# Opening tiles shared between VectorE and GpSimd and put in another order, w and u loaded as rows and transposed

## The chip, the cores and the metric

The kernel runs on one NeuronCore of one Trainium2 chip. A core has five engines that take their instructions in order and wait for each other by semaphores: TensorE (PE), VectorE (DVE), ScalarE (ACT), GpSimd (POOL) and SyncE (SP), and 16 DMA engines. The metric is the device time of one execution in microseconds (us); lower is better. Times of before are three runs and one profiled execution.

## The reference

Three stages follow one another on 3072 tokens of 384 features. The first is a linear attention with a decaying state, for 4 batches, 8 heads, 768 tokens and 48 features a head:

```python
for t in range(S):
    kt, vt, rt = (k[:, :, t], v[:, :, t], r[:, :, t])
    cur = np.einsum('bhd,bhe->bhde', u[None] * kt, vt)
    y[:, :, t] = np.einsum('bhd,bhde->bhe', rt, state + cur)
    state = w[None, :, :, None] * state + np.einsum('bhd,bhe->bhde', kt, vt)
```

w (decay, between 0.85 and 0.95) and u (bonus) have one number per head and feature, 8 x 48. The second stage is `h = x @ w_in; g = h - tanh(h); x = g @ w_out` with 2048 hidden features. The third routes each token to one of 8 experts by cosine similarity and a softmax, and gives `gate * relu(x @ w1[e]) @ w2[e]`.

## The kernel before

The tokens are cut into 24 tiles of 128, a tile object `Att(n)` for each. Attention is done by chunks of 128 tokens: within a chunk by a matrix of scores with a causal mask, between chunks by a state. Powers of w are folded into r and k first. `decay_tables` (L194) makes two tables [112 x 4 x 128] from w: squarings of w (`pw`, L196), a reciprocal, seven doublings (`tab_r`, L206) and a reversed copy on ACT (`tab_k`, L208). 112 partitions hold two heads of 48 features, one from partition 0 and one from 64; four pairs of heads lie beside each other.

The steps of one tile, by method: `products` (L376) multiplies r and k into `rows`; `summed` (L382, L384) sums it with u on PE into `ps_cd` and copies it on ACT to `cd`; `decay_r` (L355) and `decay_k` (L358) apply the tables; `scores` (L423) are 8 matmuls into `pa`, with some fill matmuls on a tile of ones ahead (`fill`, L547, whose results nobody reads); `turned` (L364) transposes k; `diagonal` (L405) makes `am` with cd on its diagonal, 8 instructions on ACT; `causal` (L428) puts the masked scores into `am` on DVE; `values` (L454) multiplies by v; `result_hi` (L459, ACT) and `result_lo` (L462, DVE) write the result in two parts.

Tiles 0 to 2 are made in an opening whose order on every engine is the order in which the code is written (`tc.manual_schedule()`), with 17 warm-up matmuls on PE (L158) ahead. Behind them come three steps (`early`, then `steps`) of the second stage woven with tiles 3 to 5, and then a long body of matmuls for stages two and three. The weights arrive as pairs of numbers in 64 bits, and are converted: bit operations on DVE (L264, L267, L270 to `wraw`), a high part on ACT (L277) and a low part on POOL (L278). One `ffn1` (L557) takes a chunk of such weights, its result `ph` is squared on ACT (`z`, L612, and `q`, L615), joined on DVE (L623, L624) and split (`ghi` L625, `glo` L635). `Logits.turn` transposes the second weights on PE (`pt`, L293) for the routing; `pst` (L475) is the state product of a tile. `IDLE` gives the number of fills ahead of `ffn1` in steps 0 to 5. All DMAs of the opening but u's two are issued by SP: w's two, the columns and rows of tiles 0 to 2 (L333, L334), then embeddings and weights.

Of the kernel before, what the change touches and what calls it, by code (L numbers as in the profile page):

```python
# [29 lines left out]
def rwkv__then__tanh_ffn__then__top1_moe_kernel(  # L30
# [56 lines left out]
    LIST = {0: (), 2: (4, 10), NB - 1: (), NB: (10,)}  # L87
    FA = 6
    START = (0, 1, 2)
    IDLE = (0, 0, 6, 4, 4, 3)  # L90
    CONV = (0, 1, 2, 3, 5, 6, 7, 8, 9, 11, 12, 13, 15, 18)
    nxt = None
    nars = {}
# [51 lines left out]
    nc.vector.memset(pw[:, :, 0:1], 0.5)  # L145
    u_pair = const.tile([PW, HP, 2], F32, name="u_pair")
    nc.vector.memset(u_pair, 0.0)
    for g in range(2):
        nc.sync.dma_start(out=pw[64 * g:64 * g + D, :, 0], in_=w.rearrange("(q g) d -> g d q", g=2)[g])
    for g in range(2):  # L150
        nc.scalar.dma_start(out=u_pair[64 * g:64 * g + D, :, g], in_=u.rearrange("(q g) d -> g d q", g=2)[g])
    ones16 = const.tile([P, P], BF16, name="ones16")
    nc.vector.memset(ones16, 1.0)

    warm = ps.tile([P, 4, P], F32, tag="p", name="warm")

    for _ in range(NWARM):
        nc.tensor.matmul(out=warm, lhsT=ones16, rhs=ones16[:, None, :].to_broadcast([P, 4, P]), start=True, stop=True)  # L158
    ident = const.tile([P, P], F32, name="ident")
    make_identity(nc, ident)  # L160
    ones_f = work.tile([P, P], F32, name="ones_f", tag="z")
    nc.gpsimd.memset(ones_f, 1.0)
    strict = work.tile([P, P], F32, name="strict", tag="q")
# [30 lines left out]
    def decay_tables(between):  # L194
        def square(i):
            nc.vector.tensor_tensor(out=pw[:, :, i + 1:i + 2], in0=pw[:, :, i:i + 1], in1=pw[:, :, i:i + 1],  # L196
                                    op=ALU.mult)

        for i in range(6):
            square(i)  # L200
        nc.vector.reciprocal(out=tab_r[:, :, 0:1], in_=w64)
        for i in range(7):
            n = 1 << i
            if i == 5:
                between()
# [1114 lines left out]
    routing_constants()  # L1320
    for x in st:
        nc.gpsimd.memset(x, 0.0)
    a[1].products(nc.vector)
    a[1].decay_r(nc.vector)
    a[1].decay_k(nc.vector)
# [36 lines left out]
    last = split(*ready[0], i=1)
# [12 lines left out]
    done.add(2)  # L1375
    early.append(ffn1([win(p, 1) for p in range(2)], columns_of(xts[0]), NK, TOK))
# [71 lines left out]
    for i in range(len(steps) + 1):  # L1448
        if i < len(steps):
            j, f = steps[i]  # L1450
            xt = xts[j]
            ph = ffn1([win(p, f) for p in range(2)], columns_of(xt), NK, TOK, IDLE[i] if i < len(IDLE) else 0) \
                if i > 1 else early[2 * i]
            if 0 in accs and spill:
                part = stage(0, [P, TB, DL], F32, "part")
                for t, x in enumerate(accs.pop(0)):
                    nc.scalar.activation(out=part[:, t, :], in_=x, func=AF.Copy)
                spill = False
            parts = squares(ph) if i > 1 else early[2 * i + 1]
# [202 lines left out]
```

## Time and profile before

| | us |
|---|---|
| median of 3 runs | 769.78 (769.21 to 770.74) |
| the profiled execution | 771.22 |
| its span in the trace | 769.6 |
| busy: PE, DVE, ACT, POOL | 756.2, 464.8, 457.1, 300.5 |

The span is the time between the first and the last instruction of the trace, and the profiled execution's own time has 1.6 us around it. PE is busy 98% of the span, warm-up and fill matmuls counted, at a mean granted clock of 0.995 of full speed.

### The profile page before, as it was taken

How to read it: one execution, taken by the hardware profiler on the slowest of the kernel's cores; microseconds unless marked ns; L12 is line 12 of the kernel's file. 1: busy time of each engine (PE TensorE's matmuls, PEld its weight loads, DVE VectorE, ACT ScalarE, POOL GpSimd, SP SyncE). 2: the span in 40 equal slices, each digit the busy share in tenths (PEclk: the TensorE clock that was granted, in tenths of full speed). 3: DMA queues.
4: the chain of work that ended last, by engine and by line, in shares of the span. 5: the costliest groups of instructions: out<-in, count | busy, mean ns of one | idle time of the engine just before them, and what ended most of it. 6: DMA issues, size and time to landing. Idle time of an engine off the chain costs nothing.

```text
span 769.6 us, 15995 instructions
## 1 busy us (share of the span) xinstructions
PE 756.2 (98%) x6143; PEld 718.4 (93%) x6143; DVE 464.8 (60%) x1037; ACT 457.1 (59%) x1064; POOL 300.5 (39%) x362
## 2 busy tenths in 40 slices
PE   9899999999999999999999999999999999999996
PEld 5689899999999999999999999999989999999996
DVE  7967976667656565565555655656684455545430
ACT  5787676655657556656657756768463535544431
POOL 3743680466781671753564341133530202110111
PEclk9899999999999999999999999999999999999999
DMA  8964355243240330232223101052374435454400
GB/s 263 288 206 142 118 170 200 64 165 100 66 148 24 126 122 2 91 94 87 80 69 123 59 32 64 14 171 85 116 229 143 129 115 189 150 173 161 154 31 32
DMA packets 41016, 92.21 MB, mean 120 GB/s; under 512 B 4827, under 2 KB 20597, under 8 KB 39907
## 3 DMA queue, kind: packets, MB, share of 16 engines
q1 hardware_dynamic: 36274, 81.44, 33.0%
q0 software_dynamic: 4240, 9.67, 3.5%
q8 instruction: 50, 0.82, 0.4%
q14 instruction: 36, 0.29, 0.1%
q10 hardware_dynamic: 416, 0.00, 0.0%
HBM read 67.26 MB, written 24.00 MB: 119 GB/s over the span
## 4 chain that ended last, share of the span: by engine, by line
PE 90%; issue 3%; DVE 3%; ACT 2%; DMA 2%; POOL 1%; POOLq 0%; SPq 0%; DVEq 0%; ACTq 0%
PE acc L572 39%; PE ph L557 37%; PE py L454 5%; PE pa L423 3%; DMA eraw<-in_moe_w_dram 2%; PE pt L908 1%; PE warm L158 1%; PE pst L475 1%; POOL out_dram L827 0%; PE pt L293 0%; DVE bits L267 0%; DVE wraw L270 0%; PE pl L303 0%; DVE bits L264 0%; PE accn L1036 0%
## 5 line engine op out<-in xcount | busy, mean ns | idle before, releaser
L557 PE MATMUL ph<-xt,wq 128*128 128x384 f32 (+4 forms) x1712 | 340.1, 341 | 1.9 <-ACT wt L295 1.3
L557 PEld LDWEIGHTS ph<-xt,wq 128*128 128x128 f32 x1712 | 302.7, 188 | 5.9 <-ACT wt L295 1.5
L572 PE MATMUL acc<-wq,ghi 128*128 128x392 f32 (+2 forms) x1120 | 289.1, 343 | 0.9 <-ACT ghi L625 0.9
L572 PEld LDWEIGHTS acc<-wq,ghi 128*128 128x128 f32 (+1 forms) x1120 | 200.3, 187 | 5.9 <-ACT ghi L625 1.2
L572 PE MATMUL acc<-wq,glo 128*128 128x392 f32 (+2 forms) x552 | 182.2, 340 | 0.1
L612 ACT ACTIVATE z<-ph 128x384 f32<-128x384 f32 x128 | 62.8, 490 | 105.0 <-PE ph L557 104.7
L623 DVE TENSOR_TENSOR ph<-ph,z 128x384 f32<-128x384 f32 x128 | 72.0, 563 | 62.6 <-ACT z L612 62.0
L572 PEld LDWEIGHTS acc<-wq,glo 128*128 128x128 f32 (+1 forms) x552 | 102.7, 187 | 0.9 <-DVE glo L635 0.7
L635 DVE TENSOR_TENSOR glo<-ph,ghi 128x384 fp32r<-128x384 f32 x128 | 70.7, 553 | 45.7 <-ACT ghi L625 45.6
L827 POOL DMA_INDIRECT out_dram<-ob,gts x27 | 27.2, 1008 | 176.6 <-ACT ob L917 171.4
L625 ACT ACTIVATE ghi<-ph 128x384 fp32r<-128x384 f32 x128 | 62.6, 490 | 41.0 <-DVE ph L624 37.6
L615 ACT ACTIVATE q<-z,sb_t 128x384 f32<-128x384 f32 x128 | 78.9, 617 | 3.4
L624 DVE SCALAR_TENSOR_TENSOR ph<-q,ph 128x384 f32<-128x384 f32 x128 | 71.7, 560 | 12.5 <-ACT q L615 3.5
L629 ACT ACTIVATE mk<-z,lz_t 128x384 bf16<-128x384 f32 x128 | 77.1, 603 | 0.0
L653 DVE SCALAR_TENSOR_TENSOR glo<-ph,ghi 128x384 fp32r<-128x384 f32 (+2 forms) x56 | 30.7, 549 | 63.8 <-ACT ghi L651 63.8
L651 ACT ACTIVATE ghi<-ph 128x384 fp32r<-128x384 f32 (+4 forms) x56 | 27.5, 491 | 67.6 <-PE ph L557 67.5
L411 POOL TENSOR_TENSOR am<-ident,cd 128x512 f32<-128x512 f32 x36 | 36.8, 1045 | 77.8 <-DVE cd L397 77.1
L886 DVE TENSOR_TENSOR wq<-eraw,wq 128x768 fp32r<-128x768 f32 x60 | 55.1, 955 | 11.5 <-ACT wq L885 11.0
L885 ACT ACTIVATE wq<-eraw 128x768 fp32r<-128x768 f32 x64 | 50.4, 839 | 6.2 <-DMA eraw<-in_moe_w_dram 6.2
L278 POOL TENSOR_TENSOR wq<-wraw,wq 128x768 fp32r<-128x768 f32 (+1 forms) x17 | 30.3, 1782 | 39.6 <-ACT wq L277 38.5
L716 POOL DMA_INDIRECT tab<-tk,irow x24 | 24.4, 1019 | 31.8 <-DVE tk L744 25.1
L491 POOL TENSOR_TENSOR st<-st,pw 112x384 f32<-112x384 f32 x20 | 16.7, 840 | 49.2 <-DVE st L484 43.7
(287 smaller groups left out, 860.0 us busy)
## 6 DMA issues: line engine op xcount, KB each, us to landing
eraw<-in_moe_w_dram SPq DMA_DIRECT2D x32, 768.0 KB, 4.5
rkv<-in_rows_dram SPq DMA_DIRECT2D x18, 640.0 KB, 5.6
tt<-in_cols_dram SPq DMA_DIRECT2D x22, 448.0 KB, 4.4
xd<-xt SPq DMA_DIRECT2D x8, 1152.0 KB, 8.0
wraw<-in_moe_w_in_dram SPq DMA_DIRECT2D x8, 768.0 KB, 8.6
wraw<-in_moe_w_out_dram SPq DMA_DIRECT2D x8, 768.0 KB, 5.2
rkv<-xe SPq DMA_DIRECT2D x22, 192.0 KB, 4.4
xe<-zero SPq DMA_DIRECT2D x2, 1536.0 KB, 15.4
```

What stands on the lines that cost most here:

```text
L454: nc.tensor.matmul(out=self.py[32 * g:32 * g + 32, kk, :], lhsT=lhs, rhs=rhs, start=start, stop=stop)
L557: mark["ph"] = nc.tensor.matmul(out=ph, lhsT=lhs[a][:, kk, :], rhs=rhs(b, kk), start=(kk == 0 and p == 0), stop=(kk == nk - 1 and p == 2)).ins
L572: mm = nc.tensor.matmul(out=acc[t][:lhs.shape[1]], lhsT=lhs, rhs=rhs(b, i), start=(i == span[0] and p == 0), stop=(i == span[1] - 1 and p ...
L612: nc.scalar.activation(out=z, in_=ph, func=AF.Square)
L615: nc.scalar.activation(out=q, in_=z, func=AF.Square, scale=SS, bias=sb_t)
L623: nc.vector.tensor_tensor(out=ph, in0=ph, in1=z, op=ALU.mult)
L624: nc.vector.scalar_tensor_tensor(out=ph, in0=q, scalar=KC, in1=ph, op0=ALU.add, op1=ALU.mult)
L625: mark["ghi"] = nc.scalar.activation(out=ghi, in_=ph, func=AF.Copy).ins
L629: nc.scalar.activation(out=mk, in_=z, func=AF.Relu, bias=lz_t, accum_out=zx[:, step:step + 1])
L635: mark["glo"] = nc.vector.tensor_tensor(out=glo, in0=ph, in1=ghi.bitcast(F32), op=ALU.subtract).ins
L885: nc.scalar.activation(out=hi[c][:, a], in_=t[:, a], func=AF.Copy)
L886: engs[s % len(engs)].tensor_tensor(out=lo[c][:, a], in0=t[:, a], in1=hi[c][:, a].bitcast(F32), op=ALU.subtract)
```

## The change

Five things change. (1) w and u are no longer loaded by element into `pw` and `u_pair`; ACT issues four loads of rows into `wu` [12 x 112], PE transposes them after 6 of the 17 warm-up matmuls, DVE copies w out of PSUM and ACT copies u. SP's first issue is then tile 0's columns. (2) The products of tiles 0 and 1, decay_k of tile 2 and decay_r of tile 3 go from DVE to POOL. (3) The opening is written in another order: decays of tiles 0 and 1 one after the other, sums of tile 2 ahead of values of tile 0, results 0 and 1 behind the third diagonal, the bit operations for the second half of the first weight behind result 2, and the embedding norms later. (4) 13 of the opening's 16 fills go, and the six of step 2. (5) The transposes of the first `Logits` move behind `ffn1` of step 2.

```diff
-    IDLE = (0, 0, 6, 4, 4, 3)
+    IDLE = (0, 0, 0, 4, 4, 3)
...
-    for g in range(2):
-        nc.sync.dma_start(out=pw[64 * g:64 * g + D, :, 0], in_=w.rearrange("(q g) d -> g d q", g=2)[g])
-    for g in range(2):
-        nc.scalar.dma_start(out=u_pair[64 * g:64 * g + D, :, g], in_=u.rearrange("(q g) d -> g d q", g=2)[g])
+    wu = work.tile([3 * HP, PW], F32, name="wu", tag="x2t")
+    nc.vector.memset(wu, 0.0)
+    nc.vector.memset(wu[:HP, D:64], 0.5)
+    for i in range(2):
+        for g in range(2):
+            nc.scalar.dma_start(out=wu[i * (g + 1) * HP:][:HP, 64 * g:64 * g + D],
+                                in_=(w, u)[i].rearrange("(q g) d -> g q d", g=2)[g])
...
+    warming(6)
     ident = const.tile([P, P], F32, name="ident")
     make_identity(nc, ident)
+    ps_wu = ps.tile([PW, 3, HP], F32, tag="p", name="ps_wu")
+    nc.tensor.transpose(ps_wu, wu, ident[:3 * HP, :3 * HP])
+    nc.vector.tensor_copy(out=pw[:, :, 0], in_=ps_wu[:, 0])
+    nc.scalar.activation(out=u_pair, in_=ps_wu[:, 1:].rearrange("p g q -> p q g"), func=AF.Copy)
+    warming(NWARM - 6)
...
-    decay_tables(lambda: a[0].products(nc.vector))
+    routing_constants()
+    decay_tables()
+    for t in a[:2]:
+        t.products(nc.gpsimd)
+    for x in st:
+        nc.gpsimd.memset(x, 0.0)
     a[0].summed()
-    a[0].decay_r(nc.vector)
-    a[0].decay_k(nc.vector)
-    a[0].scores(range(HP), 4)
+    for t in a[:2]:
+        t.decay_r(nc.vector)
+        t.decay_k(nc.vector)
+    a[0].scores(range(HP), 1)
...
     a[0].causal()
-    a[0].values(idle=2)
-    a[0].result_hi()
     a[2].products(nc.vector)
     a[2].decay_r(nc.vector)
-    a[2].decay_k(nc.vector)
+    a[2].decay_k(nc.gpsimd)
     a[2].summed()
-    a[2].scores(range(HP), 2)
+    small_constants()
     a[1].causal()
-    embedding_roots()
-    a[0].result_lo()
+    a[0].values()
     a[2].diagonal(True)
-    a[1].values(idle=3)
+    a[2].scores(range(HP))
+    a[0].result_hi()
+    a[1].values()
     a[1].result_hi()
...
     split(*ready[0], i=0)
+    a[2].values(idle=2)
+    a[1].result_lo()
+    a[2].result_hi()
+    a[2].result_lo()
+    embedding_norms()
     a.append(Att(TB, None))
     a[TB].products(nc.gpsimd)
-    a[2].values(idle=5)
-    a[1].result_lo()
-    a[2].result_hi()
-    for _ in range(2):
-        next(ops)
-    a[2].result_lo()
     for _ in ops:
         pass
...
     a[TB].decay_k(nc.gpsimd)
+    a[TB].decay_r(nc.gpsimd)
...
-    a[TB].decay_r(nc.vector)
...
+            if i == 2:
+                logits[0].turn()
+                done.add(1)
+                load_next()
```

The three places below show the order of instructions on one engine, before and after. Line numbers after the change are 7 to 10 higher for the same line. On DVE at the start of the program, before (`rows` holds the products, `tt` the columns of a tile):

```order
L171 CAST cmask<-strict 128x128
L196 TENSOR_TENSOR pw<-pw 112x4 x6
L201 RECIPROCAL tab_r<-pw 112x4
...
L376 TENSOR_TENSOR rows_162<-tt 112x512
L206 TENSOR_TENSOR tab_r<-tab_r,pw 112x4x32
L206 TENSOR_TENSOR tab_r<-tab_r,pw 112x4x64
L196 TENSOR_TENSOR pw<-pw 112x4
L355 TENSOR_TENSOR tt<-tt,tab_r 112x512
L358 TENSOR_TENSOR tt<-tt,tab_k 112x512
L376 TENSOR_TENSOR rows_162<-tt 112x512
```

and at the same place after:

```order
L167 COPY pw<-ps_wu 112x4
L180 CAST cmask<-strict 128x128
L205 TENSOR_TENSOR pw<-pw 112x4 x6
L210 RECIPROCAL tab_r<-pw 112x4
...
L213 TENSOR_TENSOR tab_r<-tab_r,pw 112x4x32
L213 TENSOR_TENSOR tab_r<-tab_r,pw 112x4x64
L205 TENSOR_TENSOR pw<-pw 112x4
L362 TENSOR_TENSOR tt<-tt,tab_r 112x512
L365 TENSOR_TENSOR tt<-tt,tab_k 112x512
L362 TENSOR_TENSOR tt<-tt,tab_r 112x512
```

The product has left the table chain, and a copy out of PSUM has come ahead of it; the mask cast stands between the copy and the squarings. On POOL in the opening, after (`tk` and `zero` are constants, `st` the states, `first` the columns of tile 2):

```order
L1288 IOTA tk_163 128x48
L383 TENSOR_TENSOR rows_167<-tt 112x512
L1293 MEMSET zero 128x384
L383 TENSOR_TENSOR rows_167<-tt 112x512
L1325 MEMSET st_130 128x384
...
L365 TENSOR_TENSOR first<-first,tab_k 112x512
L285 TENSOR_TENSOR wq_75<-wraw,wq_72 128x384
L383 TENSOR_TENSOR rows_167<-tt 112x512
```

Before, the memsets followed `tk` directly, and the first multiplication on POOL was the low part of the first weight; the two products and decay_k of `first` are new there. On PE at step 2, before:

```order
L364 MATMUL ps_k<-ident,tt 128x112 x4
L293 MATMUL pt<-ident,wraw 128x128 x6
L547 LDWEIGHTS ones_94
L547 MATMUL ph<-ones_94 128x384
L547 LDWEIGHTS ones_94
L547 MATMUL ph<-ones_94 128x384
```

and after:

```order
L371 MATMUL ps_k<-ident,tt 128x112 x4
L564 MATMUL ph<-xt,wq_72 128x384 x2
L564 MATMUL ph<-xt,wq_75 128x384
...
L300 MATMUL pt<-ident,wraw 128x128 x6
L482 MATMUL pst<-first,ktok 48x48 x8
```

The transposes of `wraw` and the fills stood ahead of step 2's `ffn1`; now `ffn1` follows the turn of k directly and the transposes stand behind it.

## Rows read from the trace of the kernel before

**Rows 1.** Windows: stretch, length, busy us (instructions), granted PE clock, DMA share, GB/s.
```profile
core 0: us, PE busy (x) PEld busy (x) DVE busy (x) ACT busy (x) POOL busy (x), PEclk, DMA share, GB/s
0.00:21.30 21.30, 19.44 (x209) 12.42 (x209) 16.60 (x47) 12.23 (x35) 7.41 (x47) 1.00 0.89 264
21.30:37.70 16.40, 13.53 (x100) 11.04 (x101) 16.29 (x35) 12.75 (x35) 12.78 (x10) 0.79 0.99 299
37.70:51.20 13.50, 13.18 (x161) 10.85 (x160) 10.12 (x22) 13.27 (x39) 3.72 (x2) 1.00 0.54 150
...
110.00:769.00 659.00, 652.56 (x5182) 630.33 (x5180) 374.45 (x832) 378.37 (x863) 242.07 (x277) 1.00 0.33 108
```

**Rows 2.** Timeline of the start (start, us, engine, line), and DMA issues to landing.
```profile
1.08 0.89 SPq L149 DMA_DIRECT2D pw<-in_w_dram  x2
1.12 0.89 ACTq L151 DMA_DIRECT2D u_pair<-in_u_dram  x2
1.30 6.64 PE L158 MATMUL warm<-ones 128*128 128x512 bf16 x17 [1.30 <-DVE ones L153]
2.05 0.34 DVE L171 CAST cmask<-strict 128x128 uint8<-128x128 f32 x1 [0.80 <-POOL strict L164]
4.08 1.17 DVE L196 TENSOR_TENSOR pw<-pw 112x4 f32<-112x4 f32 x6 [1.70 <-DMA pw<-in_w_dram]
...
tt<-in_cols_dram SPq DMA_DIRECT2D x2, 448.0 KB, 4.0
...
DMA to landing us min/median/max: 2.4/2.5/2.6
```

**Rows 3.** Timeline: products on DVE and POOL, and tab_k.
```profile
6.48 0.68 DVE L376 TENSOR_TENSOR rows<-tt 112x512 f32<-112x512 f32 x1
7.86 0.63 ACT L208 ACTIVATE tab_k<-tab_r 112x512 f32<-112x512 f32 x1 [4.53 <-DVE tab_r L206]
...
21.85 1.30 POOL L376 TENSOR_TENSOR rows<-tt 112x512 f32<-112x512 f32 x1 [0.47 <-DMA tt<-in_cols_dram]
```

**Rows 4.** decay_r on DVE (ns min/median/max), and decays beside each other on POOL and DVE.
```profile
L355 DVE TENSOR_TENSOR tt<-tt,tab_r x4: 674/692/1402, 7.9 to 31.8; 112x512 f32<-112x512 f32 x4
...
31.33 1.29 POOL L358 TENSOR_TENSOR tt<-tt,tab_k 112x512 f32<-112x512 f32 x1
31.77 1.40 DVE L355 TENSOR_TENSOR tt<-tt,tab_r 112x512 f32<-112x512 f32 x1
```

**Rows 5.** Timeline: one tile's scores, turn, sums and diagonal.
```profile
10.42 0.60 PE L364 MATMUL ps_k<-ident,tt 112*128 112x112 f32 x4
10.86 0.96 PE L382 MATMUL ps_cd<-u_pair,rows 112*128 112x2 f32 x8
11.75 1.16 PE L423 MATMUL pa<-tt 48*128 48x128 f32 x16
...
15.81 0.18 ACT L384 ACTIVATE cd<-ps_cd 128x8 f32<-128x8 f32 x1 [0.41 <-PE ps_cd L382]
16.02 2.45 ACT L405 ACTIVATE am<-ident,cd 128x128 f32<-128x128 f32 x8
```

**Rows 6.** Timeline: embedding norm's power and bit operations in the opening.
```profile
15.75 0.58 POOL L1247 TENSOR_TENSOR en_n<-en_n,half 8x1 f32<-8x1 f32 x1 [8.99 <-DVE en_n L1246]
16.06 0.54 DVE L264 TENSOR_SCALAR bits<-wraw 128x384 int32<-128x384 int32 x1
```

**Rows 7.** Timeline: the waits of ACT and DVE in step 2, and one join.
```profile
37.70 0.90 ACT L277 ACTIVATE wq<-wraw 128x768 fp32r<-128x768 f32 x1 [1.99 <-DVE wraw L270]
...
39.33 0.18 DVE L1260 COPY ent<-ps_en 128x24 f32<-128x24 f32 x1 [1.67 <-PE ps_en L1259]
39.42 0.56 DVE L623 TENSOR_TENSOR ph<-ph,z 128x384 f32<-128x384 f32 x1
```

**Rows 8.** Windows of 2 us with the granted clock, and ffn1 of steps 2 and 3.
```profile
30.00:32.00 2.00, 0.43 (x2) 0.43 (x3) 2.00 (x5) 2.00 (x8) 1.89 (x2) 0.72 1.05 392
32.00:34.00 2.00, 1.14 (x6) 0.73 (x5) 2.00 (x3) 2.00 (x8) 2.00 (x2) 0.50 1.03 394
...
35.73 2.79 PE L557 MATMUL ph<-xt,wq 128*128 128x384 f32 x9
...
44.09 1.89 PE L557 MATMUL ph<-xt,wq 128*128 128x384 f32 x9
```

More of the change, by code (lines that the diff above doesn't have):

```diff
@@ L144, in rwkv__then__tanh_ffn__then__top1_moe_kernel @@
     pw = const.tile([PW, HP, 8], F32, name="pw")
-    nc.vector.memset(pw[:, :, 0:1], 0.5)
     u_pair = const.tile([PW, HP, 2], F32, name="u_pair")
-    nc.vector.memset(u_pair, 0.0)
-    for g in range(2):
-        nc.sync.dma_start(out=pw[64 * g:64 * g + D, :, 0], in_=w.rearrange("(q g) d -> g d q", g=2)[g])
-    for g in range(2):
-        nc.scalar.dma_start(out=u_pair[64 * g:64 * g + D, :, g], in_=u.rearrange("(q g) d -> g d q", g=2)[g])
+    wu = work.tile([3 * HP, PW], F32, name="wu", tag="x2t")
[5 more added lines that the diff above has]
+                                in_=(w, u)[i].rearrange("(q g) d -> g q d", g=2)[g])
     ones16 = const.tile([P, P], BF16, name="ones16")
@@ L155, in rwkv__then__tanh_ffn__then__top1_moe_kernel, with warming @@
     warm = ps.tile([P, 4, P], F32, tag="p", name="warm")
-    for _ in range(NWARM):
-        nc.tensor.matmul(out=warm, lhsT=ones16, rhs=ones16[:, None, :].to_broadcast([P, 4, P]), start=True, stop=True)
+    def warming(n):
+        for _ in range(n):
+            nc.tensor.matmul(out=warm, lhsT=ones16, rhs=ones16[:, None, :].to_broadcast([P, 4, P]), start=True, stop=True)
+    warming(6)
     ident = const.tile([P, P], F32, name="ident")
     make_identity(nc, ident)
+    ps_wu = ps.tile([PW, 3, HP], F32, tag="p", name="ps_wu")
[3 more added lines that the diff above has]
+    warming(NWARM - 6)
     ones_f = work.tile([P, P], F32, name="ones_f", tag="z")
@@ L192, in small_constants, with decay_tables @@
         nc.vector.memset(ent, 0.0)
-    def decay_tables(between):
+    def decay_tables():
         def square(i):
@@ L203, in decay_tables @@
             n = 1 << i
-            if i == 5:
-                between()
             nc.vector.tensor_tensor(out=tab_r[:, :, n:2 * n], in0=tab_r[:, :, 0:n],
@@ L1312, in rwkv__then__tanh_ffn__then__top1_moe_kernel @@
     a = [Att(n, xts[0]) for n in range(TB)]
-    decay_tables(lambda: a[0].products(nc.vector))
+    routing_constants()
[4 more added lines that the diff above has]
+        nc.gpsimd.memset(x, 0.0)
     a[0].summed()
-    a[0].decay_r(nc.vector)
-    a[0].decay_k(nc.vector)
-    a[0].scores(range(HP), 4)
+    for t in a[:2]:
+        t.decay_r(nc.vector)
+        t.decay_k(nc.vector)
+    a[0].scores(range(HP), 1)
     a[0].turned()
     a[0].diagonal(True)
[L1320 to L1325, printed above, removed]
     a[1].summed()
@@ L1329, in rwkv__then__tanh_ffn__then__top1_moe_kernel @@
     a[1].diagonal(True)
-    small_constants()
-    embedding_norms()
     a[0].causal()
-    a[0].values(idle=2)
-    a[0].result_hi()
     a[2].products(nc.vector)
     a[2].decay_r(nc.vector)
-    a[2].decay_k(nc.vector)
+    a[2].decay_k(nc.gpsimd)
     a[2].summed()
-    a[2].scores(range(HP), 2)
+    small_constants()
     a[1].causal()
-    embedding_roots()
-    a[0].result_lo()
+    a[0].values()
     a[2].diagonal(True)
-    a[1].values(idle=3)
+    a[2].scores(range(HP))
+    a[0].result_hi()
+    a[1].values()
     a[1].result_hi()
@@ L1349, in rwkv__then__tanh_ffn__then__top1_moe_kernel @@
     a[2].causal()
+    a[0].result_lo()
     next(ops)
     split(*ready[0], i=0)
+    a[2].values(idle=2)
[3 more added lines that the diff above has]
+    embedding_norms()
     a.append(Att(TB, None))
     a[TB].products(nc.gpsimd)
-    a[2].values(idle=5)
-    a[1].result_lo()
-    a[2].result_hi()
-    for _ in range(2):
-        next(ops)
-    a[2].result_lo()
     for _ in ops:
         pass
+    embedding_roots()
     last = split(*ready[0], i=1)
@@ L1490, in rwkv__then__tanh_ffn__then__top1_moe_kernel @@
             logits.append(Logits(c, ready[2 * c + 1][0]))
-            logits[c].turn()
-            done.add(2 * c + 1)
+            if c:
+                logits[c].turn()
+                done.add(2 * c + 1)
         if m < NF:
```

## The prediction

> **What bounds the kernel now.** I read the table of windows first, with borders at the end of the hand-ordered opening (21.3 us), at the second weight conversion of step 2 on ACT (37.7 us) and at the point from which PE is hardly ever idle (51.2 us) [rows 1]. From 110 us to the end PE is busy 652.56 of 659 us at the full granted clock. The change touches nothing there, so whatever it moves before about 51 us comes through to the end whole, as an earlier or later start of a PE-bound body. Before that the limits differ by stage. To 21.3 us PE works 19.44 us, but a part of that is warm-up and fill matmuls. From 21.3 to 37.7 us DVE is busy 16.29 of 16.40 us: DVE sets the pace, and a microsecond that DVE starts later or gets more of is a microsecond. From 37.7 to 51.2 us ACT is busy 13.27 of 13.50 us and PE 13.18.
>
> Then I read the timeline of the opening, to see what each engine waits for. DVE starts the six squarings of the decay at 4.08 us, once the last load of w has landed; the tables are its only work, apart from tile 0's products [rows 2, 3]. ACT sits idle 4.53 us until tab_k at 7.86 us. From then on ACT makes three diagonals of 2.45 us each with short waits between them for PE's small sums (0.41 us before the third), and the third ends at 16.02 + 2.45 = 18.47 us [rows 3, 5]. Causal mask, values, result and the first ffn1 follow from that.
>
> **The loads and the tables.** Before, two loads on SP and two on ACT run side by side. After, ACT issues four. Two issues take 0.89 us there and begin at 1.12 us, so the fourth begins at about 1.12 + 3 × 0.445 = 2.45 us, and with 2.5 us to landing (2.4 to 2.6 for u) it lands at 4.95 us [rows 2]. The new loads have rows of 48 floats in place of single elements; a landing 0.7 us sooner is my optimistic end, since no row shows such a small load landing under 2 us. The transpose costs about 0.15 (a quarter of the four in ps_k, 0.60), the copy 0.18 (as the ent copy), and the mask cast, which DVE now does between copy and squares, 0.34 [rows 2, 5, 7]. Squares start at about 5.65 with a hand-over, say 5.7, in place of 4.08. The table chain ran from 4.08 to 7.86 with one product of 0.68 in it, that is 0.60 by start to start, so 3.16 us without it. Undisturbed it ends at 5.7 + 3.16 = 8.9: 1.0 us later than before, the saved product included.
>
> **The products on POOL.** A product takes 1.30 us on POOL against 0.68 on DVE [rows 3]. SP's first issue is now tile 0's columns: 1.08 + 4.0 = 5.1 us landed, and POOL makes product 0 from 5.1 to 6.4 us [rows 2]. Product 1 follows behind a memset, in any case before the tables end. So both lie beside DVE's table work. What that costs is the disputed price. The trace has one clear place: decay_r of 112x512 takes 0.69 us (median of four), but 1.40 us where it began 0.44 us into a POOL multiplication of the same shape [rows 4]. It lost 0.71 us of the 0.85 that POOL still had to run, nearly the whole of it. The bounds are therefore zero (the small 112x4 operations slip in between) and a full block: 0.7 us for product 0 (5.7 to 6.4) and 1.3 for product 1, together 2.0. I take the full price, because the one place where two such streams meet shows it. Tables then end at 8.9 + 2.0 = 10.9, 3.0 us later than tab_k began before.
>
> The Trainium skill, page "SBUF — State Buffer", section "Who interferes with whom", speaks against this part of the change: a DVE instruction with two SBUF inputs and a GpSimd instruction that reads SBUF exclude each other, the second to issue blocks fully, and issue order rather than shape decides who blocks. By that rule small operations are no way out, and the sum would be the one with 2.0; the trace agrees for the large shape (1.40 against 0.69), and no run here shows it yet for 112x4.
>
> **From the tables to the third diagonal.** Decays r and k of tile 0 are 2 × 0.69 behind the tables (tab_k's 0.63 beside the first): scores 0 at 12.3. PE then needs scores 1.16, ps_k 0.60 and ps_cd 0.96 before ACT can start cd of tile 1: 12.3 + 2.72 = 15.0; its diagonal, with cd, takes 2.45 + 0.18: 17.7. In the new order the sums of tile 2 stand on PE directly behind tile 1's scores and turn (15.0 + 2.72 = 17.7), not behind values 0, so the third diagonal ends at 17.7 + 2.65 = 20.35 instead of 18.47: **+1.9 us** [rows 5]. The removed fills cost or give nothing here: PE waits for tables in their place. The product of tile 2 and its decay_r fit on DVE while ACT works; decay_k of tile 2 on POOL takes 1.3 us while PE does tiles 0 and 1, and is covered so long as it is done by about 16 us.
>
> **DVE behind the opening.** Before, the bit operations on the second half of the first weight (L264, L267) sat in DVE's wait for result 2. Now they stand behind it: 2 × 0.54 = 1.1 us. The embedding norms also come later: DVE's part, 0.1, and a power of 0.58 on POOL that DVE then waits for, of which I count 0.5. Against it, decay_r of tile 3 leaves DVE (0.67, about 0.6 by start to start) [rows 4, 6]. Net **+1.1 us**, in the stretch in which DVE has no idle time to swallow it.
>
> **Step 2.** Six fills go, and the six weight transposes move behind ffn1. PE had sat there waiting for DVE's wraw, the granted clock fell to 0.72 and 0.50 of full speed, and ffn1 took 2.79 us instead of 1.89 [rows 8]; ACT waited 1.99 us for wraw and DVE 1.67 for what came after [rows 7]. After, ffn1 no longer waits for the transposes, so its z and what follows can fill ACT's wait. At most 1.99 us come back. At the low end DVE now has to fit two operations of 0.56 (L623, L624 of step 2) ahead of that same wraw, which leaves 1.99 − 1.1 = 0.9. I take **−1.2 us**, nearer to the low end, since DVE is the engine that this stretch waits for [rows 1].
>
> Sum: 1.9 + 1.1 − 1.2 = +1.8 us. The profiled execution took 771.22 us (span 769.6), so 773.0; it stood 1.44 above the median of 769.78, so the median should be **771.6 us**. From there the PE-bound body keeps the shift.
>
> **The rivals.** Faster or slower by 0.2% is 1.54 us, about what a measurement of this kernel can tell from no change: below 768.24 or above 771.32.
>
> A, the forecast: POOL's products stretch the tables. 771.6, own range 770.6 to 772.6. Chance 0.40.
>
> B: the block does not bite, because small operations slip past or the products start outside the tables. Tables end at 8.9, decays at 10.3; but PE's eleven warm matmuls behind the transpose, at 6.64 / 17 = 0.39 each, end at 5.1 + 4.3 = 9.4, then ps_cd 0.96 and one fill, so scores 0 at 10.6. Twice 2.72 gives sums of tile 2 at 16.05, third diagonal at 18.75: +0.3. With +1.1 and −1.2 the sum is +0.2: 770.0. For it: the table operations last only 0.16 to 0.4 us, and the trace shows the block on longer ones. Chance 0.25.
>
> C, the other side: ACT's diagonals set the opening and nothing else does. If the row loads land by about 4.2 us and nothing blocks, squares start by 4.9, warm-up ends at 4.2 + 0.15 + 4.3 = 8.65, cd 0 starts at 9.6 at the latest, and three diagonals back to back take 3 × 2.63 = 7.9: they end at 17.5, or 17.1 if PE hands over sooner, because the 0.4 us waits of ACT for the sums are gone with the sums of tile 2 moved forward. That is −1.0 to −1.4 against 18.47. ACT then also takes its whole 1.99 in step 2: −1.1 + 1.1 − 2.0 = −2.0, so 767.8. It decides from the point at which the tables end before about 8.2 us. Against it: four issues in a row on one queue. Chance 0.20.
>
> D: the clock. PE idles from 1.30 + 6 × 0.39 = 3.6 to 5.0 us for the transpose and from about 10.4 to 12.3 for the late scores, with fewer fills. In the trace, where PE had 0.43 us of work in 2 us, the clock fell, and one ffn1 cost 0.9 us more [rows 8]. Once or twice that on top of A: 772.5 to 773.4, middle 773.0. Chance 0.15.
>
> **Range and chances.** A lies around the upper bound, more above it (0.26) than within (0.14). B: 0.18 same, 0.04 faster, 0.03 slower. C: 0.15 faster, 0.05 same. D: slower. So faster 0.19, same 0.37, slower 0.44. The range runs from just under C's value to D's upper end, 767.6 to 773.4; it leaves out half of C's spread and the far tail of D, some 0.17.
>
> **What would show it.** In the changed trace: squares starting near 5.7 (if under 4.9, C lives); table operations on DVE with an idle or stretched time of 0.7 and 1.3 us exactly beside POOL's two products (if each keeps its 0.16 to 0.4 us, B); third diagonal ending near 20.4; the first ffn1 near 23.2 instead of 21.35; granted clock 1.00 through the opening (else D); no window at half clock around 32 to 37 us, and z of step 3 some 1.8 us later than before. I am wrong if the block is a matter of large shapes only, if the loads by rows land much faster, or if the bit operations find another gap on DVE.

## The result and the profile after

The changed kernel took 778.32 us (median of 6 runs, 776.42 to 781.10), the kernel before 769.50 on the same chip (6 runs): ratio 1.0111, 95% interval 1.0085 to 1.0136. It is slower by 8.8 us, where 1.8 was forecast. The profiled execution took 781.10 us (span 779.4) and is the slowest of the six, so its trace shows more loss than the median run has. Runs of this kernel spread over 4.7 us and the mean granted clock of a run goes from 0.982 to 0.993, the lowest of them in the slowest run.

The windows of the profile after, cut at scores 0 (14.9 us), the first ffn1 (31.2, the place of the first border of [rows 1]) and z of step 3 (57.3):

```profile
core 0: us, PE busy (x) PEld busy (x) DVE busy (x) ACT busy (x) POOL busy (x), PEclk, DMA share, GB/s
8.50:14.90 6.40, 4.20 (x18) 2.11 (x16) 5.91 (x19) 1.32 (x5) 1.74 (x5) 0.77 1.03 357
14.90:31.20 16.30, 15.71 (x170) 13.65 (x170) 9.07 (x21) 8.97 (x30) 2.11 (x2) 0.58 0.82 235
31.20:57.30 26.10, 21.89 (x179) 18.69 (x183) 22.18 (x49) 21.04 (x58) 19.22 (x14) 0.87 0.48 147
57.30:110.00 52.70, 51.04 (x501) 47.08 (x501) 43.83 (x95) 37.89 (x94) 25.45 (x20) 1.00 0.47 146
```

Scores 0 start at 14.9 us, and the first ffn1 comes 16.3 us behind them, at a mean granted clock of 0.58. In the windows of before the same two points lie 12.0 us apart, at full clock:

```profile
9.30:21.30 12.00, 11.44 (x181) 8.84 (x180) 11.20 (x25) 9.88 (x32) 1.53 (x2) 1.00 1.03 322
21.30:46.00 24.70, 21.81 (x185) 17.77 (x189) 21.88 (x47) 20.88 (x56) 14.63 (x11) 0.86 0.81 240
```

So by the first ffn1 the loss is 31.2 − 21.3 = 9.9 us, of which 5.6 lie ahead of scores 0 and 4.3 behind them. Another 1.4 comes in steps 2 and 3 (26.1 against 24.7). From z of step 3 on the shift stays: 46.04 to 57.30, and 53.66 to 64.90 for the next one. The end is only 9.8 us later, since PE's wait behind late expert weights near 521 us of before (0.9 us) is not there after; the other 0.5 us lie in the same 20 us and were not followed further. That wait comes and goes with runs of either kernel: in the twenty profiles PE waits 0 to 1.2 us there, and from z of step 3 to the end it takes between 721.75 (e5) and 724.50 us (e9), 723.56 in before. So z of step 3 shows what the opening costs more cleanly than the end of one execution does.

The start of the program, as timeline of after (start, us, engine, line), answers to [rows 2, 3]; the last line is a piece of the chain of work (start, us, what).

```profile
1.19 0.85 ACTq L151 DMA_DIRECT2D wu<-in_w_dram  x2
2.06 0.66 ACTq L151 DMA_DIRECT2D wu<-in_u_dram  x2
7.37 0.19 PE L166 MATMUL ps_wu<-ident,wu 12*112 12x12 f32 x1 [3.14 <-DMA wu<-in_u_dram]
7.55 1.26 POOL L383 TENSOR_TENSOR rows<-tt 112x512 f32<-112x512 f32 x1 [0.96 <-DMA tt<-in_cols_dram]
7.68 2.65 DVE L180 CAST cmask<-strict 128x128 uint8<-128x128 f32 x1
8.75 1.49 POOL L1325 MEMSET st<- 128x384 f32 x4
13.48 0.63 ACT L215 ACTIVATE tab_k<-tab_r 112x512 f32<-112x512 f32 x1 [5.51 <-DVE tab_r L213]
14.89 2.08 PE L430 MATMUL pa<-tt 48*128 48x128 f32 x16 [2.20 <-DVE tt L365]
...
2.40 4.83 DMA wu<-in_u_dram
```

Three things are to be seen. The fourth load was issued at 2.40 us, as forecast (2.45), but took 4.83 us to land, not 2.5; tile 0's 448 KB, issued at 0.92, and three more loads that SP had issued by then were ahead of it. The cast took 2.65 us, not 0.34: POOL's product 1 and the four memsets of `st` lie beside it, and it ends when the last memset does. And PE waited 2.20 us for the scores' operand, after which the same 16 matmuls took 2.08 us instead of 1.16.

The clock in windows around that wait:

```profile
12.00:14.00 2.00, 0.70 (x6) 0.45 (x5) 1.83 (x7) 0.52 (x1) 0.00 (x0) 1.00 1.06 386
14.00:16.00 2.00, 1.10 (x10) 1.11 (x12) 2.00 (x4) 1.90 (x8) 0.00 (x0) 0.72 0.90 351
16.00:28.00 12.00, 12.00 (x106) 10.77 (x108) 5.36 (x15) 5.67 (x21) 1.72 (x1) 0.50 0.76 221
```

PE was idle for 2.2 us, then the granted clock fell from 2.4 to 1.2 GHz, and stayed there for at least 12 us in which PE was busy without a gap. In those 12 us everything of the opening stands behind PE. (The 0.77 ahead of scores 0 in the first table is an earlier fall, to 0.51 from 8 to 10 us, behind PE's 3.14 us wait for the transpose. It met the warm-up; PE was through with its sums and its fill at 12.70 us, before the scores' operand was there.)

### The profile page after: what moved, and what is told of

It reads as the page before. It is cut to its first block, busy times and chain, and to the rows that moved or that the text cites. A ratio compares the mean times of both kernels' runs of the same rounds, so it can differ in the third digit from the quotient of the medians.

```text
span 779.4 us, 15967 instructions
## 1 busy us (share of the span) xinstructions
PE 760.0 (98%) x6125; PEld 724.1 (93%) x6125; DVE 464.9 (60%) x1034; ACT 456.7 (59%) x1065; POOL 306.5 (39%) x366
## 4 chain that ended last, share of the span: by engine, by line
PE 90%; issue 3%; DVE 3%; DMA 1%; ACT 1%; POOL 1%; ACTq 0%; POOLq 0%; DVEq 0%
PE acc L579 39%; PE ph L564 38%; PE py L461 5%; PE pa L430 4%; PE pt L915 1%; PE pst L482 1%; PE pt L300 1%; DMA wu<-in_u_dram 1%; DMA eraw<-in_moe_w_dram 1%; PE pl L310 1%; PE ps_cd L389 1%; POOL out_dram L834 0%; DVE bits L274 0%; DVE wraw L277 0%; PE ps_k L371 0%
## 5 line engine op out<-in xcount | busy, mean ns | idle before, releaser
L435 DVE COPY_PREDICATED am<-cmask,pa 128x512 f32<-128x512 uint8 x48 | 33.0, 733 | 6.5 <-PE pa L430 4.8
## 6 DMA issues: line engine op xcount, KB each, us to landing
xd<-xt SPq DMA_DIRECT2D x8, 1152.0 KB, 11.9
```

## Experiments

All ratios are to the kernel before on the same chip, from 4 to 12 runs a kernel. The table gives the ratio with its interval, and from each profile the starts of the first ffn1 and of z of step 3 (before 21.35 and 46.04, after 31.21 and 57.30). It lies near the ratio of the mean times, so a long run moves it: e12 has 1.0073, but 1.0054 by its medians, with one run of seven at 781.08 us; e7 has 1.0045, and 1.0066 by its medians.

| run | ratio | first ffn1 | z of step 3 |
|---|---|---|---|
| e1_w_first | 1.0080 (1.0067 to 1.0093) | 26.52 | 52.54 |
| e2_cast_early | 1.0075 (1.0052 to 1.0098) | 25.32 | 51.32 |
| e3_products_dve | 1.0095 (1.0080 to 1.0110) | 25.28 | 51.31 |
| e4_step2_as_before | 1.0115 (1.0100 to 1.0129) | 31.13 | 56.25 |
| e5_before_step2 | 0.9997 (0.9985 to 1.0009) | 21.23 | 46.95 |
| e6_elements | 1.0049 (1.0032 to 1.0066) | 25.53 | 51.47 |
| e7_three | 1.0045 (1.0024 to 1.0065) | 24.93 | 51.37 |
| e8_three_fills | 1.0050 (1.0032 to 1.0067) | 30.08 | 54.53 |
| e9_fills | 1.0086 (1.0067 to 1.0105) | 27.16 | 51.70 |
| e10_before_less_fill | 1.0003 (0.9985 to 1.0021) | 25.81 | 50.06 |
| e11_before_products | 1.0025 (1.0005 to 1.0044) | 21.77 | 46.09 |
| e12_before_rows | 1.0073 (1.0047 to 1.0099) | 25.84 | 50.87 |
| e13_more_warm | 1.0039 (1.0025 to 1.0054) | 22.30 | 47.73 |
| e14_order | 1.0005 (0.9996 to 1.0013) | 21.74 | 47.10 |
| e15_before_hold | 1.0007 (0.9998 to 1.0016) | 21.43 | 45.87 |
| e16_late_and_lock | 1.0084 (1.0070 to 1.0097) | 26.96 | 52.43 |
| e17_rows_on_sp | 1.0078 (1.0058 to 1.0097) | 27.66 | 53.73 |
| e18_step2_held | 0.9984 (0.9970 to 0.9997) | 21.37 | 43.95 |

**The late loads.** Four runs change part (1) alone, e1 and e17 only the issue of its loads, e6 and e12 the transpose and the warm-up in two parts too; three are on the changed kernel and one on the kernel before.

```diff
# e1_w_first: SP issues w's rows ahead of tile 0's columns
-            nc.scalar.dma_start(out=wu[i * (g + 1) * HP:][:HP, 64 * g:64 * g + D],
+            (nc.sync, nc.scalar)[i].dma_start(out=wu[i * (g + 1) * HP:][:HP, 64 * g:64 * g + D],
# e17_rows_on_sp: SP issues all four
+            nc.sync.dma_start(out=wu[i * (g + 1) * HP:][:HP, 64 * g:64 * g + D],
# e6_elements: loads by element into pw and u_pair as before, no transpose, 17 warm-up matmuls in a row
# e12_before_rows: the kernel before with the new loads, transpose and warm-up in two parts
```

> The changed kernel with w's two row loads issued by SP ahead of tile 0's columns and u's two by ACT; nothing else differs. Late load (the small loads wait 4.83 us behind SP's big ones): the last row lands near 4.1 us instead of 7.23, squares start near 5, tables end between 8.2 and 9.7 instead of 13.5, the first ffn1 starts near 22 to 24 instead of 31.2, time 769 to 772. Lock (POOL's products hold DVE off wherever the tables lie): tables shift by the same 3 us only, the stretched 2.5 us moves to another table operation, time 774 to 776. Clock alone (too few fills): half clock stays from the first scores on, time above 775.

> The changed kernel with all four row loads issued by SP, one after the other, ahead of tile 0's columns; nothing else differs. If the big loads ahead make the small ones late: the last row lands near 4.8 us (issue near 2.3, 2.5 to landing) in place of 7.23, squares start near 5.4, ratio 1.004 to 1.009 as in the run with w first. If four issues in a row on one queue make them late: landing near 7 and ratio 1.010 or more.

> The changed kernel with part (1) undone: w by element on SP ahead of tile 0's columns, u by element on ACT, no transpose, 17 warm-up matmuls in a row; POOL's products, order, fills and step 2 stay changed. Late load as the main cause: squares at 4.1 us, tables end near 8.7 (one block of 1.3 by product 0), and the ratio falls from 1.011 to 1.000 to 1.004. Lock and missing fills as main causes: tables near 9.5, PE idle ahead of scores 0, half clock behind it, ratio 1.006 to 1.009.

> The kernel before with part (1) alone: w and u by rows from ACT, the transpose, tile 0's columns leading SP; products stay on DVE, fills and order as before. Late load alone: the last row lands near 7.2, squares start near 7.9 with the cast at its 0.15 to 0.34 us, scores 0 start near 13.2, and since PE has its eleven late warm-up matmuls and the fills in between the clock stays: ratio 1.004 to 1.006. If the row load is late only with POOL's products beside it: landing near 5, ratio 1.000 to 1.002.

In e17 the four issues stand in a row on one queue, the last at about 2.3 us as in the changed kernel, but ahead of the columns. Its timeline:

```profile
1.18 0.73 SPq L151 DMA_DIRECT2D wu<-in_w_dram  x2
1.96 0.63 SPq L151 DMA_DIRECT2D wu<-in_u_dram  x2
2.63 0.32 SPq L340 DMA_DIRECT2D tt<-in_cols_dram  x1
...
4.16 0.23 PE L166 MATMUL ps_wu<-ident,wu 12*112 12x12 f32 x1
```

The transpose starts at 4.16 us, right behind the six warm-up matmuls and without a wait for a load. So the last of them, issued at about 1.96 + 0.63 / 2 = 2.28, had landed at most 1.9 us later, and it was not the four issues but the big loads ahead. Nor was it ACT's queue: in e1 ACT issues u's rows, the second at about 1.6 us, tile 0's columns follow on SP at 1.96, and the transpose does not wait either (4.15 us). e12 shows the same from the other side, in a kernel in which POOL reads nothing there: issued at 2.40 us, landed 5.54 us later, as the chain has it.

```profile
2.40 5.54 DMA wu<-in_u_dram
...
8.38 0.22 DVE L180 CAST cmask<-strict 128x128 uint8<-128x128 f32 x1
8.52 1.17 DVE L205 TENSOR_TENSOR pw<-pw 112x4 f32<-112x4 f32 x6
```

With late loads alone, transpose and warm-up in two parts included, z of step 3 is 4.8 us later, and the ratio 1.0073. The queueing was shown by the order of issue; how the engines share packets among queues was not measured. e1 (777.18 us, where 769 to 772 was expected) and e6 (1.0049, where 1.000 to 1.004 was) did not come down to what the late-load theory alone expected; e17 lies within its range, and e12 above it with an interval that reaches into it. In e1, e6 and e17 PE still waited ahead of scores 0 (2.81, 2.19 and 2.30 us), and the clock fell in the opening.

**DVE and POOL.** Three runs take the overlap away or bring it alone.

```diff
# e2_cast_early: the cast of cmask stands ahead of the copy of w
+    nc.vector.tensor_copy(out=cmask, in_=strict)
     nc.vector.tensor_copy(out=pw[:, :, 0], in_=ps_wu[:, 0])
# e3_products_dve
-    for t in a[:2]:
-        t.products(nc.gpsimd)
...
+    a[0].products(nc.vector)
...
+    a[1].products(nc.vector)
# e11_before_products: the kernel before with
+    for t in a[:2]:
+        t.products(nc.gpsimd)
```

> The changed kernel with DVE's mask cast ahead of the copy of w out of PSUM, so that it runs near 2 us; nothing else differs. Lock: the cast takes 0.34 us again, the first square now waits for product 1 (to 8.8 us) and the memsets do not stretch it, tables end near 12.0 instead of 13.5, time 776 to 777. If memsets on POOL hold DVE off as well, the first square is stretched as the cast was, tables end at 13.3 and the time stays at 778. Late load alone: 778.

> The changed kernel with products 0 and 1 on DVE, each ahead of its tile's decays, and POOL's memsets directly behind the constants; nothing else differs. Lock: cast and squares are no longer stretched (0.34 and 1.17 us), tables end near 11.2, and with the product on DVE the scores start near 13.4 instead of 14.9: time 776 to 777. Late load alone: scores 0.7 later than in the changed kernel, time 778 to 779.

> The kernel before with products 0 and 1 on POOL ahead of its memsets, the fills kept; loads, order and step 2 as before. Lock: product 0 lies at 6.0 to 7.3 beside the last table operations and holds one of them to its end, product 1 at 8.9 to 10.2 does the same to a decay, and scores 0 start at 9.8 to 10.2 instead of 9.3; with PE's fills as cover the ratio is 0.999 to 1.002. No lock: scores 0 start at 8.7, ratio 0.998 to 1.000.

In e1 the tables are early and still beside the products. Two single operations of its timeline, each with the product that lies beside it:

```profile
5.62 1.26 POOL L383 TENSOR_TENSOR rows<-tt 112x512 f32<-112x512 f32 x1 [0.29 <-DMA tt<-in_cols_dram]
5.68 1.22 DVE L205 TENSOR_TENSOR pw<-pw 112x4 f32<-112x4 f32 x1
...
8.09 1.26 POOL L383 TENSOR_TENSOR rows<-tt 112x512 f32<-112x512 f32 x1 [1.21 <-DMA tt<-in_cols_dram]
8.25 1.25 DVE L213 TENSOR_TENSOR tab_r<-tab_r,pw 112x128 f32<-112x128 f32 x1
```

A square of 112x4 that takes 0.17 us alone took 1.22, until the product was over; a doubling of 112x128 that takes 0.29 took 1.25. Together that is 2.0 us, the full price that I had taken: small operations are held like large ones. In e2 the cast ran at 2.05 us in 0.33, and the squares met product 1 and then the memsets:

```profile
7.49 1.26 POOL L383 TENSOR_TENSOR rows<-tt 112x512 f32<-112x512 f32 x1 [0.75 <-DMA tt<-in_cols_dram]
7.84 1.94 DVE L205 TENSOR_TENSOR pw<-pw 112x4 f32<-112x4 f32 x6
8.69 1.49 POOL L1325 MEMSET st<- 128x384 f32 x4
9.81 0.18 DVE L210 RECIPROCAL tab_r<-pw 112x4 f32<-112x4 f32 x1
```

Six squares take 1.17 us in e12 and 1.94 here: 0.8 us longer, which is what was left of the product (8.75 − 7.84 = 0.91, less what one square does in it). The memsets, from 8.69 to 10.18, cost them nothing. So the cast, with one input, is held by product and memset, and a square, with two inputs, by the product alone. In e9 and e16, with the same order on both engines, the cast did not wait for the last memset: it ended at 9.66 and 9.31 us, and there the four memsets took 1.57 us instead of 1.49, until 10.37 and 10.03. The Trainium skill, page "SBUF — State Buffer", section "Who interferes with whom", has both halves: an operation with two SBUF inputs is in the way of a GpSimd instruction that reads SBUF, not of one that only writes, and a DVE instruction in a two-port mode, which a copy or a cast can enter, of any. The trace agrees with it on both counts (1.94 against 1.17, 2.65 against 0.22); that the cast runs in such a mode is not in the trace. e3, without products on POOL, has the cast at 0.22 us and scores 0 at 13.16 instead of 14.89; e2 has them at 13.33. In the times neither run is clear of the changed kernel: the intervals of 1.0075 and 1.0095 overlap with its 1.0085 to 1.0136. z of step 3 comes 6 us sooner in both profiles, but most of that is the clock: from scores 0 to the first ffn1 they take 12.0 and 12.1 us against 16.3. It is down for about 3 us there and for 13 in the profile after, and it falls near 18 us, with PE busy since scores 0, so not every fall stands right behind a wait.

e11 brings the products alone to the kernel before: scores 0 start at 9.71 instead of 9.33 and z of step 3 is where it was, with a ratio of 1.0025 that its interval hardly sets apart from 1. With the tables early, the price does not reach z.

**The clock.** Five runs change what PE does while it waits.

```diff
# e9_fills: the changed kernel with fills 12, 2, 2, 3, 5 (e10: the kernel before with 1, 0, 0, 0, 2)
-    a[0].scores(range(HP), 1)
+    a[0].scores(range(HP), 12)
# e7_three: e1, e2 and e3 together; e8_three_fills: and fills 4, 2, 2, 3, 5
# e13_more_warm: e8 with step 2 as before, and
-    warming(NWARM - 6)
+    warming(20)
```

> The changed kernel with the opening's fills put back (2, 2, 3, 5) and 12 fills ahead of scores 0, enough to cover PE's wait for the late tables; loads, products and order stay as changed. Clock: tables still end near 13.5 and scores 0 start near 14.9, but no half clock follows, so from scores 0 to the first ffn1 it takes 12 to 12.7 us as before instead of 16.3, first ffn1 near 27.3, ratio 1.005 to 1.008. If the clock does not matter there (ACT or DVE set the pace): first ffn1 stays past 30, ratio 1.010 to 1.012.

> The kernel before with the opening's fills cut as in the change (1, 0, 0, 0, 2); nothing else differs. If the fills alone hold the clock: half clock appears between 12 and 20 us, first ffn1 at 23 or later instead of 21.35, ratio 1.002 to 1.006. If the clock falls only with the late tables: clock stays at 1.00, PE gets up to 2 us ahead and waits, first ffn1 at 20.5 to 21.4, ratio 0.998 to 1.000.

> The changed kernel with three edits at once: w's row loads on SP ahead, the mask cast ahead of the copy, products 0 and 1 on DVE. Late load and lock together: squares at 4.6 with 1.17 us, tables end near 7.9, scores 0 near 9.9, first ffn1 near 21.5 to 22.5, ratio 1.000 to 1.003. If missing fills alone suffice for the fall of the clock: scores start early, but half clock appears between 12 and 22 us, first ffn1 after 24, ratio above 1.005.

> The changed kernel with w's row loads on SP ahead, the mask cast early, products 0 and 1 on DVE, and the opening's fills as before (4, 2, 2, 3, 5); left of the change are row loads with the transpose, the order, and step 2. If late load, lock and clock are the whole loss of the opening: squares near 4.6, scores 0 near 10.0, no half clock to 25 us, first ffn1 near 21.5 to 22.3, z of step 3 near 47 to 48, ratio 1.000 to 1.003. If the new order itself costs something: first ffn1 past 23, ratio 1.004 to 1.006.

> The kernel of e8_three_fills (w's loads ahead, cast early, products on DVE, fills as before) with 20 instead of 11 warm-up matmuls behind the transpose and step 2 as before; left of the change are row loads with the transpose and the order. If the clock explains the rest: PE has no gap of over 1 us ahead of scores 0, full clock to 25 us, first ffn1 near 21.5 to 22.5, ratio 0.999 to 1.002. If the order costs something by itself: first ffn1 past 23 at full clock, ratio 1.003 or more.

Windows of e9, from the warm-up to scores 0, from there to the first ffn1, and on to z of step 3:

```profile
8.90:15.20 6.30, 6.30 (x29) 3.32 (x27) 5.82 (x20) 2.28 (x8) 1.47 (x4) 1.00 1.05 373
15.20:27.10 11.90, 11.35 (x181) 8.77 (x180) 8.37 (x19) 7.93 (x26) 2.43 (x2) 1.00 0.82 221
27.10:51.70 24.60, 20.72 (x179) 17.79 (x183) 22.27 (x49) 21.14 (x58) 17.00 (x14) 0.93 0.60 181
```

Scores 0 are as late as ever, but PE was busy through the wait, the clock is at 1.00 from there on, and the stretch to ffn1 took 11.9 us instead of 16.3. That settles 4.3 us of the profile on the clock. The 1.00 of the first row is not to be trusted for the warm-up, which does not run faster there than in the changed kernel at 0.51 (the first line is e9, the second after):

```profile
8.00:10.00 2.00, 2.00 (x6) 0.75 (x5) 1.91 (x4) 0.07 (x1) 2.00 (x5) 1.00 1.05 297
8.00:10.00 2.00, 2.00 (x7) 0.69 (x6) 2.00 (x2) 0.00 (x0) 2.00 (x5) 0.51 0.96 263
```

From scores 0 on the matmuls bear it out: the sixteen take 1.16 us, as before.

In the times e9's 1.0086 against 1.0111 lies within the intervals. The clean pair is e4 and e16, which differ in fills alone: 1.0115 (1.0100 to 1.0129) and 1.0084 (1.0070 to 1.0097), 0.3% or 2.4 us apart, z of step 3 at 56.25 and 52.43, and a mean granted clock of 0.983 to 0.988 in e4's four runs, of 0.992 to 0.995 in e16's five. The same stretch of the opening in e4 and in e16, where PE gets through 36 and 79 instructions:

```profile
20.00:24.00 4.00, 4.00 (x36) 3.70 (x38) 2.47 (x4) 1.63 (x6) 0.15 (x1) 0.50 0.95 264
20.00:24.00 4.00, 4.00 (x79) 2.77 (x81) 2.75 (x5) 2.89 (x11) 0.05 (x1) 1.00 0.93 267
```

The clock does not fall in every execution. Of e10's twelve (768.6 to 774.2 us) two, at 774.2 and 774.0, have a mean granted clock of 0.984 and 0.985, the other ten 0.990 to 0.995. Three of those ten took 772.3 to 774.1 all the same, as four of 25 runs of before did on that chip (772.3 to 773.3), so the clock is not the whole of the spread. e10's profile is the slowest run and has half clock from 12 to 24 us:

```profile
8.00:10.00 2.00, 1.19 (x17) 0.94 (x18) 1.97 (x4) 1.90 (x7) 0.00 (x0) 1.00 1.09 258
10.00:12.00 2.00, 2.00 (x22) 1.88 (x18) 2.00 (x9) 1.16 (x4) 0.00 (x0) 0.82 1.00 236
12.00:14.00 2.00, 2.00 (x17) 1.91 (x17) 1.97 (x4) 1.72 (x7) 0.00 (x0) 0.50 1.06 390
```

There PE had waited 0.60 us for the product and 0.81 ahead of scores 0, with one fill in place of four. So with these fills cut the clock fell in some executions and not in others, and the ratio of 1.0003 shows no cost in the mean. e7, too without them, has four runs with a mean granted clock of 0.991 to 0.993, three of them at 769.9 to 770.3 us, and seven with 0.984 to 0.987, at 773.4 to 776.4. With fills (e8) six of seven are at 0.992 to 0.995, and take 771.7 to 775.1; in e8's profile, its slowest run, PE waited 1.85 us for product 0 behind its shorter warm-up and the clock fell for the whole opening. With nine more warm-up matmuls (e13) it stayed at 1.00 to 30 us, and the first ffn1 came at 22.30. Its ratio of 1.0039 is above what its z of step 3 (+1.7 us, 0.2%) says; where the rest lies I have not settled.

**Step 2, and the order.** Five runs.

```diff
# e4_step2_as_before: the changed kernel without the hunks for IDLE and logits[0].turn()
# e5_before_step2: the kernel before with both; e18_step2_held: with the second, IDLE[2] = 6, and in turn()
+                fill(pt, 0 if self.c else 4)
# e15_before_hold: the kernel before with fills of 9 and 5 there, IDLE[2] = 2
# e14_order: the changed kernel with loads, products, fills and step 2 as before
# e16_late_and_lock: the changed kernel with e9's fills and step 2 as before
```

> The changed kernel with step 2 as before (six fills, transposes ahead of ffn1); nothing else differs. As forecast in the prediction, step 2 gives 0.9 to 2.0 us back, so without its change the time rises to 779 to 780.5. Rival: the moved transposes make PE wait for the results of the diagonal instead, so that the clock falls there (0.50 from 50 to 55 us), and without the change the time falls by 1 to 2 us, to 776.5 to 777.5.

> The kernel before with step 2's change alone (no fills there, transposes behind ffn1). My prediction's term: 0.9 to 2.0 us faster, ratio 0.9975 to 0.999. Rival, from the runs so far (first ffn1 to z of step 3 took 26.0 us with the change of step 2 and 25.1 without it): 1 us slower at z of step 3, ratio 1.000 to 1.002.

> The kernel before with step 2's transposes behind its ffn1, the six fills ahead of ffn1 kept, and four more ahead of each half of the transposes. If the change of step 2 is worth something with the clock held: no window under 0.9 between 30 and 46 us, z of step 3 at 45.3 to 45.6 instead of 46.04, ratio 0.9985 to 0.9997. If the clock falls all the same, or ACT and DVE set the pace: z of step 3 at 46 to 47, ratio 0.9997 to 1.002.

> The kernel before with fills ahead of step 2's transposes (9 and 5) and 2 instead of 6 ahead of its ffn1, so that PE is busy from 29.7 to 35 us. If the fall of the clock there costs time: ffn1 of step 2 takes 1.9 us instead of 2.8, z of step 3 comes 0.5 to 1.0 us sooner, ratio 0.9985 to 0.9995. If ACT and DVE set the pace there: z of step 3 at 46.0, ratio 0.9995 to 1.0005.

> The changed kernel with loads, products of tiles 0 and 1, fills and step 2 as before; what is left is the new order, decay_k of tile 2 and decay_r of tile 3 on POOL. My prediction's term for DVE behind the opening is +1.1 us and the third diagonal no later than before: ratio 1.001 to 1.002. The rival by which sums of tile 2 ahead of values 0 free ACT: third diagonal ends up to 1.4 us sooner, ratio 0.998 to 1.000.

> The changed kernel with 12 fills ahead of scores 0, the other fills as before, and step 2 as before; loads, products and order stay changed. If the parts add up: z of step 3 some 4.5 us later than before (5.5 with the fills alone, 1.0 less for step 2), ratio 1.005 to 1.007. If step 2's change matters only when the clock falls in the opening: 5.5 us, ratio 1.007 to 1.009.

In the profiles of the changed kernel and of e5, step 2's part makes z of step 3 later, by 57.30 − 56.25 = 1.05 and 46.95 − 46.04 = 0.91 us. The times show neither: 1.0111 with it and 1.0115 without (e4), and 0.9997 for e5. ffn1 of step 2 itself comes sooner, as meant, but PE then waits for DVE, 1.63 and 0.65 us for `causal`, and the clock falls at the scores and transposes ahead of ffn1 of step 3. From the windows of after:

```profile
50.00:52.00 2.00, 2.00 (x16) 1.48 (x17) 2.00 (x6) 1.99 (x8) 1.86 (x1) 0.50 0.80 316
52.00:54.00 2.00, 2.00 (x19) 1.52 (x11) 2.00 (x4) 1.77 (x6) 0.00 (x0) 0.50 0.02 8
54.00:56.00 2.00, 2.00 (x8) 1.50 (x7) 0.11 (x1) 1.32 (x4) 1.52 (x1) 0.54 0.29 36
```

PE is full there and DVE at the end nearly idle. e18 keeps six fills ahead of that ffn1 and puts four ahead of each half of the transposes. Its window of the same work, from the first ffn1 to z of step 3, and z itself:

```profile
21.30:43.90 22.60, 20.41 (x197) 17.07 (x201) 21.42 (x47) 20.70 (x56) 14.64 (x11) 1.00 0.83 249
...
43.95 0.51 ACT L613 ACTIVATE z<-ph 128x384 f32<-128x384 f32 x1
```

The clock never falls, and the stretch takes 22.6 us instead of 24.7 ([rows 8] are the half clock that it had before). z of step 3 is 2.1 us sooner in this profile, one of two executions of twelve with a mean granted clock of 0.999 (the others have 0.993 to 0.997), and the ratio 0.9984 (0.9970 to 0.9997): a little faster than both kernels. e15 adds fills around the old order and holds the clock only in part (0.69 in the mean from 32 to 36 us, 0.50 before); it moved z by 0.17 us and the time not at all, though its ffn1 of step 2 took 1.88 us instead of 2.79. So the move did not gain without the fills, nor these fills without the move; the two together did. The order alone (e14) costs 1.06 us at z and 0.05% of the time, which is within the noise. Its third diagonal ends at 16.16 + 2.45 = 18.61 us, against 18.47 before.

## Why the prediction was wrong

The direction was right; the size, 8.8 us against 1.8, was not, and 778.3 lies above the range (773.4). By the prediction's own steps, from before by way of e14, e16 and e4 to the changed kernel, at z of step 3 of the profiles: order 47.10 − 46.04 = 1.1 us, late loads and lock with the clock held 52.43 − 47.10 = 5.3, the missing fills and with them the clock 56.25 − 52.43 = 3.8, step 2 57.30 − 56.25 = 1.05; together 11.3. The ratios of the same four are 1.0005, 1.0084, 1.0115 and 1.0111: the loads and the lock are most of it, the clock 0.3%, and order and step 2 not apart from nothing.

**The loads and the tables** is the step that failed first. "With 2.5 us to landing (2.4 to 2.6 for u) it lands at 4.95 us": it landed at 7.23. I took the landing time from a trace in which the small loads stood ahead of the big ones [rows 2], and weighed the number of issues on ACT but not the change by which tile 0's 448 KB come first. e17 and e12 show it, and e12's 4.8 us at z are most of the 5.3. In the same step the cast was priced at 0.34 and took 2.65, since I thought of POOL's reads only and not of what its memsets do to a cast; e2 shows it.

**The products on POOL**: the price of 2.0 us was right (2.0 in e1), so the mechanism of case A holds, also for small operations. In the changed kernel the tables were so late that product 0 missed them, and product 1 with the memsets hit the cast instead. What is left for it at z is about 5.3 − 4.8 = 0.5 us, an estimate from e16, e14 and e12. "Tables then end at 10.9": at 13.5.

**From the tables to the third diagonal** and rival D: "the removed fills cost or give nothing here: PE waits for tables in their place" is the second step that failed. They cost, because PE idle ahead of the scores took the clock down for 12 us and more. I had this as rival D, at 0.9 to 1.8 us on top of A and a chance of 0.15. The price came from one ffn1 at half clock; but the opening is a row of PE work that others wait for, and at half clock it cost 4.3 us in the profile by the first ffn1, 3.8 at z and 2.4 in the times by e4 and e16.

**DVE behind the opening**, +1.1: e14 has the whole new order, the moved bit operations and norms among it, and z of step 3 is 1.06 us later. That it agrees is in part luck: 0.39 us of it are there by the first ffn1, ahead of the stretch that was meant, and its parts were not traced.

**Step 2**, −1.2: at z sign and size depend on the clock. As the change has it, +0.9 to +1.05, of which the times show nothing; with the clock held, −2.1 in the profile, just over the upper bound of 1.99 that I had given, and 0.16% (0.03 to 0.30) in the times. The work that fills ACT's wait was there, as the prediction said; what was missing is that PE would wait behind it in other places.

Rival C is dead by e14: tab_k starts at 7.44 us there, ahead of its 8.2, and the third diagonal did not end sooner. B is dead by the 1.22 us square of e1. "From there the PE-bound body keeps the shift" held to 0.02 us from z of step 3 to the next; by the end of the profile 1.4 us of 11.3 were gone.

## What to carry to other kernels

A few hundred bytes that gate the first computation belong ahead of the big loads across all queues, and the time to landing of a load is only worth quoting together with what stands ahead of it. Work is not free on GpSimd while DVE runs a short serial chain, and memsets count too where DVE casts. Before fills are cut or work is moved away ahead of a wait, look at what PE does in that wait: here half clock for 12 us followed one wait of 2 us, and the same move in step 2 put z 2 us sooner with the clock held and 1 us later without. How much of such a difference in two profiles is there in the times has to be asked of the times.

## What the runs showed of the hardware

A small load of 0.8 KB took 2.2 to 2.6 us to land by elements with nothing ahead of it, at most 1.9 by rows (e17), and 4.83 and 5.54 by rows behind 448 KB and more from another queue. A cast of 128x128 on DVE was held by GpSimd memsets that only write (2.65 us against 0.22), where multiplications with two inputs were not. And whether the clock falls behind a short wait of PE differs between executions of one program on one chip: e10 took 768.6 us in one run, at a mean granted clock of 0.993, and 774.2 in another, at 0.984. The granted clock of a window can read 1.00 while matmuls run at half pace: six warm-up matmuls in 2 us of e9, against seven at 0.51 in the changed kernel.
